# Reordering the twelve S1 T1 matmuls in one stage of a seven-product MLP kernel

## The chip, the cores and the metric

The kernel runs on one core of a Trainium2 chip. The metric is the device time of one execution in microseconds (us), lower is better. A change of 0.2% of this time is 1.15 us.

## The reference, cut to what matters

```python
# attention: linear attention with decay, in blocks; its output becomes x
x = attn_out.transpose(0, 2, 1, 3).reshape(1536, 512)
# first MLP ("layer 0"), d_model 512, d_ff 2048
h = np.maximum(x @ w_in, 0.0)
x = h * h @ w_out
# second MLP ("layer 1"), weights of the same shapes
h = x @ w_in2
out = np.maximum(0.01 * h, h) @ w_out2
```

Weights come as 64-bit floats and are turned into 32-bit ones on the chip.

## The kernel before, in words

Every 32-bit operand of a matmul is held as two parts, `hi` and `lo` (`split`: a cast on ScalarE, then a subtraction on VectorE), and a product is three matmuls: hi by hi, hi by lo, lo by hi. `three` (L562) issues them all, so nearly all TensorE rows of the trace have that line; the rows are told apart by the tiles they read.

The 1536 tokens are three tiles of 512 (t = 0, 1, 2). The hidden width of 2048 is cut into four stages (s = 0 to 3) of 512. A stage makes the hidden values of its 512 columns (`first`, the tiles g0 and g1 with parts h and l), multiplies them by its rows of the second weight, and adds the result into an accumulator in DRAM (`spill`). In the second and third stage of the first MLP, s = 1 and s = 2 (`seven`), the second matmul of the token tiles 0 and 1 is done by `second_pair` with seven block products in place of eight. The products are named by their operands: A11 B11, S1 T1, A12 B21, S4 B22, S2 T2, A22 T4, S3 T3. B and T are blocks of hidden values or differences of such blocks, A is a block of weights and S a sum of weight blocks (tile `sw` on the chip). Each product is done for two output halves p = 0, 1, and each half is six matmuls: two row blocks of hidden values (h = 0, 1) by three.

The order of the products on TensorE is the order in which the program is written. PSUM banks are named A, B, C, D per p. S1 T1 starts bank C, and S4 B22 adds to bank C later; in between, ScalarE must have copied bank C to SBUF (`keep`, L684), because the result of S1 T1 alone is wanted too. From SBUF the copy is added to DRAM by an accumulating DMA that POOL issues (L688), or stored by SP.

T1 is in g1: hi and lo of row block h = 0 come early, those of h = 1 come last, out of a chain on VectorE (L550, difference; L69, lo part) and ScalarE (L68, cast). After S1 T1, `late_split` writes T3 over T1 in the same tiles: a cast on ScalarE and a subtraction on VectorE for each h, at raised priority. The block T2 (tile `t4`, shown as `t`) is cast by L68 after VectorE's L455. ScalarE, VectorE and POOL get their order from a scheduler that goes by the program's dependences; each engine then runs its list strictly in order.

After the seven products, POOL also adds stored partial results to others in DRAM (L758): each waits for an earlier DMA of the same data. At the same time `converting` turns weights into 32-bit parts on ScalarE and VectorE (L115 to L138), each fed by a 1 MB load `raw` that SP issues as soon as VectorE's L123 has freed a buffer.

Of the kernel before, what the change touches and what calls it, by code (L numbers as in the profile page):

```python
# [19 lines left out]
def tile_retention_then_two_mlps(  # L20
# [16 lines left out]
    C = P  # L37
# [20 lines left out]
    def bank():  # L58
        return psum.tile([P, 512], F32, tag="ps", name="ps")

    def plain():
        return fp.tile([P, TT], F32, tag="f", name="f")

    def dma(dst, src):
        return nc.sync.dma_start(dst, src)

    def split(hi, lo, src):
        nc.scalar.copy(hi, src)  # L68
        nc.vector.tensor_tensor(out=lo, in0=src, in1=hi, op=ALU.subtract)  # L69
# [19 lines left out]
    wts, sums, opened = {}, {}, set()  # L89
# [470 lines left out]
    def three(ps, ops, start, stop, again=False):  # L560
        for n, (a, b) in enumerate(ops):
            nc.tensor.matmul(ps, a, b, start=start and n == 0, stop=stop and n == len(ops) - 1, skip_group_check=again)  # L562

    def first(l, s, t, ms=range(KF)):
        for m in ms:
            if m == 0:
                new_g(l, s, t)
            ghi, glo = g[t]
            hi, lo = wts[l, s, 0, m // 2]
            cs = slice(m % 2 * P, (m % 2 + 1) * P)  # L570
            ps = bank()
            ops = []
            for kk in range(KD):
                ops += [(hi[:, kk, cs], xhi[t][:, kk]), (hi[:, kk, cs], xlo[t][:, kk]), (lo[:, kk, cs], xhi[t][:, kk])]
            three(ps, ops[:6], True, False)
            yield True
            three(ps, ops[6:], False, True)
            if (l, s) in seven and t < 2:
                activate_for_seven(t, m, ps)
            elif (l, s) == stages[-1]:  # L580
                activate_last(t, m, ps)
                if m == KF - 1:
                    sums_last(t)
            else:
                activate(l, ps, plain(), ghi[:, m], glo[:, m])
            if t == 2 and m % 2:
                opened.add((*stages[stages.index((l, s)) + 1], 0, m // 2) if (l, s) != stages[-1] else None)
            yield True
# [93 lines left out]
    def keep(src, dst, first):  # L682
        f = plain()
        nc.scalar.copy(f, src)  # L684
        if first:
            dma(dst, f)
        else:
            nc.gpsimd.dma_start(dst, f, accum_op=ALU.add)  # L688
# [3 lines left out]
    def second_pair(s):  # L692
        partial = partials[s]
        (g0h, g0l), (g1h, g1l) = g[0], g[1]
        x = {
            "B11": [(g0h[:, 2 * h], g0l[:, 2 * h]) for h in range(2)],
            "B21": [(g0h[:, 2 * h + 1], g0l[:, 2 * h + 1]) for h in range(2)],
            "B22": [(g1h[:, 2 * h + 1], g1l[:, 2 * h + 1]) for h in range(2)],
            "T1": [(g1h[:, 2 * h], g1l[:, 2 * h]) for h in range(2)],
            "T2": [(tt[2][:, 0, h], tt[2][:, 1, h]) for h in range(2)],  # L700
        }
        ps = {}

        def product(p, where, a, b, start=True):
            if start:
                ps[p, where] = bank()
            ops = []
            for h in range(2):
                if a[0] == "A":
                    i, j = int(a[1]) - 1, int(a[2]) - 1  # L710
                    hi, lo = (w[:, j, (2 * p + i) * P:(2 * p + i + 1) * P] for w in wts[0, s, 1, h])
                else:
                    hi, lo = (sums[0, s, 1, h][:, part, int(a[1]) - 1, p] for part in range(2))
                bh, bl = x[b][h]
                ops += [(hi, bh), (hi, bl), (lo, bh)]
            three(ps[p, where], ops, start, True, not start)
            return ps[p, where]

        def kept(p, i, k):
            return spill[0][k][2 * p + i]  # L720

        def late_split(n, old, m):
            x[n] = x[old]
            with tc.high_priority(offset=400):
                for h in range(2):
                    split(*x[n][h], later[m(h)])

        both = range(2)
        for p in both:
            keep(product(p, "A", "A11", "B11"), partial[p]["P1"], True)  # L730
            yield True
        for p in both:
            keep(product(p, "C", "S1", "T1"), kept(p, 1, 1), False)
            yield True
        late_split("T3", "T1", lambda h: (1, 2 * h))
        for p in both:
            keep(product(p, "A", "A12", "B21", False), kept(p, 0, 0), False)
            yield True
        late_split("T4", "B21", lambda h: (0, 2 * h + 1))
        for p in both:  # L740
            keep(product(p, "C", "S4", "B22", False), kept(p, 0, 1), False)
            yield True
        for p in both:
            keep(product(p, "B", "S2", "T2"), partial[p]["P6"], True)
            yield True
        for p in both:
            keep(product(p, "D", "A22", "T4"), kept(p, 1, 0), False)
            yield True
        yield from first(0, s, 2)
        for p in both:  # L750
            keep(product(p, "B", "S3", "T3", False), partial[p]["P67"], True)
            yield True
        opened.add(("sums", 0, s + 1))
        for p in both:
            p1, p6, p67 = (partial[p][n] for n in ("P1", "P6", "P67"))
            for dst, src in ((p67, p1), (kept(p, 0, 1), p1), (kept(p, 0, 1), p6), (kept(p, 1, 0), p67),
                             (kept(p, 1, 1), p67)):
                nc.gpsimd.dma_start(dst, src, accum_op=ALU.add, max_dma_last_dim=TT)  # L758
# [136 lines left out]
    def stage(l, s):  # L895
        if (l, s) == (0, 0):
            parts = [first(l, s, t, range(2)) for t in range(NTILE)]
            parts += [first(l, s, t, range(2, 4)) for t in (0, 2, 1)]
            return parts + [second(l, s, t) for t in (2, 0, 1)]
        if l == 0:  # L900
            parts = [first(l, s, t, ms) for ms in (range(2), range(2, 4)) for t in range(2)]
        else:
            parts = [first_pair(s)]
        if (l, s) in seven:
            return parts + [second_pair(s), second(l, s, 2)]
        if (l, s) == (0, NS - 1):
            return parts + [second(l, s, 0), second(l, s, 1, (0, 2, 1)), first(l, s, 2), second(l, s, 1, (3,)),
                            second(l, s, 2)]
        if (l, s) == stages[-1]:
            return parts + [first(l, s, 2)] + [second_last(s, t) for t in range(NTILE)]  # L910
        return parts + [second(l, s, 0), first(l, s, 2), second(l, s, 1), second(l, s, 2)]
# [36 lines left out]
```

## Time and profile before

| what | value |
|---|---|
| device time, median of 3 runs (lowest, highest) | 573.77 us (573.05, 574.43) |
| profiled execution: device time, span of the trace | 575.28 us, 573.5 us |
| granted TensorE clock, mean | 0.999 |
| TensorE busy | 562.3 us, 98% of the span |
| VectorE, ScalarE, POOL busy | 441.1, 312.9, 112.5 us |
| TensorE idle after 100 us, all two waits | 1.5 us |

Times in rows count from the start of the span. In a row of a timeline the columns are start, duration, engine, line, operation, output<-inputs, count, and in brackets the idle time before it with what ended it. A row with "x2" merges two instructions, and the time between them is in its duration. Two matmuls in a row overlap, so durations are longer than the distance of their starts.

### The profile page before, as it was taken

Reading aid. Unit: us, or ns where it says so; the run is one execution under the profiler, and the core shown is the slowest. Engines: PE = TensorE matmul, PEld = TensorE weight load, DVE = VectorE, ACT = ScalarE, POOL = GpSimd, SP = SyncE. Lnnn points to the kernel's source line nnn. Section 1 sums busy time; section 2 is a strip of 40 time slices with the busy share of each in tenths; the row PEclk is TensorE's granted clock in tenths of the full one; section 3 lists DMA queues with packets and bytes.
Section 4 is the critical chain, followed back from the end, with each engine's and each line's share of the span. In section 5 each row is a group of like instructions: output and inputs, shape, how many; then the busy total and the mean of one; then the engine's idle time right before and its main releaser. Section 6 shows DMA issues by size and latency. Waiting matters only on the chain.

```text
span 573.5 us, 8321 instructions
## 1 busy us (share of the span) xinstructions
PE 562.3 (98%) x3171; PEld 473.3 (83%) x3171; DVE 441.1 (77%) x623; ACT 312.9 (55%) x494; POOL 112.5 (20%) x121
## 2 busy tenths in 40 slices
PE   7989999999999999999999999999999999999997
PEld 6879888888788887888888888888888888888897
DVE  3678999999927589498478999929875395918887
ACT  2344598556758677657538474543662375435610
POOL 3749100000044603434000000000203111220032
PEclk9999999999999999999999999999999999999999
DMA  8998434665589966999602225362439406460434
GB/s 176 233 216 174 151 125 142 223 191 176 181 148 146 137 193 155 218 242 200 194 8 88 76 69 196 110 209 74 64 84 240 54 7 141 59 89 2 155 140 147
DMA packets 80760, 80.77 MB, mean 141 GB/s; under 512 B 40264, under 2 KB 54608, under 8 KB 80720
## 3 DMA queue, kind: packets, MB, share of 16 engines
q1 hardware_dynamic: 62576, 62.01, 35.2%
q0 software_dynamic: 17472, 17.83, 22.7%
q8 instruction: 25, 0.41, 0.3%
q10 hardware_dynamic: 672, 0.39, 0.2%
q14 instruction: 15, 0.12, 0.1%
HBM read 55.05 MB, written 30.42 MB: 149 GB/s over the span
## 4 chain that ended last, share of the span: by engine, by line
PE 74%; DVE 11%; DMA 8%; ACT 3%; issue 2%; POOL 1%; SPq 0%; ACTq 0%; POOLq 0%; DVEq 0%
PE ps L562 69%; DMA raw<-in_moe_w_in 5%; DMA raw<-in_moe_w_out 2%; DVE rb L123 2%; DVE hb L119 2%; PE ps L298 1%; DVE hb L126 1%; ACT hb L115 1%; PE ps L315 1%; DVE rb L122 1%; DVE hb L116 1%; DMA q<-in_q 1%; PE ps L366 1%; PE ps L224 1%; PE ps L364 1%
## 5 line engine op out<-in xcount | busy, mean ns | idle before, releaser
L688 POOL DMA_DIRECT2D spill<-f x48 | 47.5, 1200 | 348.4 <-ACT f L684 348.3
L562 PE MATMUL ps<-xhi,w1h 128*128 128x512 f32 x288 | 112.2, 389 | 0.0
L562 PE MATMUL ps<-xlo,w1h 128*128 128x512 f32 x288 | 112.1, 389 | 0.0
L562 PE MATMUL ps<-xhi,w1l 128*128 128x512 f32 x288 | 112.0, 389 | 0.0
L684 ACT COPY f<-ps 128x512 f32<-128x512 f32 x84 | 48.4, 586 | 65.4 <-PE ps L562 64.5
L562 PEld LDWEIGHTS ps<-xhi,w1h 128*128 128x128 f32 x288 | 54.1, 188 | 11.3 <-issue 0.2
L562 PEld LDWEIGHTS ps<-xhi,w1l 128*128 128x128 f32 x288 | 54.1, 188 | 11.3
L562 PEld LDWEIGHTS ps<-xlo,w1h 128*128 128x128 f32 x288 | 54.1, 188 | 11.2
L115 ACT ACTIVATE hb<-raw 128x1024 f32<-128x1024 f32 x32 | 36.7, 1148 | 25.9 <-DMA raw<-in_moe_w_in 9.4
L479 DVE TENSOR_TENSOR g0l<-f,g0h 128x512 fp32r<-128x512 f32 x44 | 29.7, 687 | 25.4 <-ACT f L475 20.6
L138 DVE TENSOR_TENSOR w2l<-hb,w2h 128x1024 fp32r<-128x1024 f32 x16 | 19.5, 1223 | 29.5 <-ACT w2h L136 29.5
L562 PE MATMUL ps<-g0h,w2h 128*128 128x512 f32 x104 | 40.5, 389 | 0.0
L562 PE MATMUL ps<-g0l,w2h 128*128 128x512 f32 x104 | 40.5, 389 | 0.0
L562 PE MATMUL ps<-g0h,w2l 128*128 128x512 f32 x104 | 40.5, 389 | 0.0
L123 DVE SCALAR_TENSOR_TENSOR rb<-raw,rb 128x1024 f32<-128x1024 uint32 x32 | 39.4, 1232 | 0.4
L126 DVE TENSOR_TENSOR hb<-hb,rb 128x1024 f32<-128x1024 f32 x32 | 39.4, 1232 | 0.3
L562 PE MATMUL ps<-w2l,g0h 128*128 128x512 f32 (+1 forms) x104 | 39.6, 381 | 0.0
L562 PE MATMUL ps<-w2h,g0l 128*128 128x512 f32 (+1 forms) x104 | 39.6, 381 | 0.0
L562 PE MATMUL ps<-w2h,g0h 128*128 128x512 f32 (+1 forms) x104 | 39.6, 381 | 0.0
L119 DVE SCALAR_TENSOR_TENSOR hb<-raw,hb 128x1024 uint32<-128x1024 uint32 x32 | 39.1, 1221 | 0.4
L634 DVE TENSOR_TENSOR f<-ps,f 128x512 f32<-128x512 f32 x40 | 26.3, 685 | 10.7 <-PE ps L562 10.4
L116 DVE TENSOR_SCALAR hb<-hb 128x1024 f32<-128x1024 f32 x32 | 23.0, 718 | 12.4 <-ACT hb L115 12.1
(209 smaller groups left out, 1234.0 us busy)
## 6 DMA issues: line engine op xcount, KB each, us to landing
raw<-in_moe_w_in SPq DMA_DIRECT2D x16, 1024.0 KB, 5.7
raw<-in_moe_w_out SPq DMA_DIRECT2D x16, 1024.0 KB, 5.6
spill<-f POOLq DMA_DIRECT2D x48, 256.0 KB, 6.2
spill<-f SPq DMA_DIRECT2D x24, 256.0 KB, 2.5
k<-in_k SPq DMA_DIRECT2D x12, 256.0 KB, 4.9
q<-in_q SPq DMA_DIRECT2D x12, 256.0 KB, 5.1
v<-in_v SPq DMA_DIRECT2D x12, 256.0 KB, 5.1
f<-spill SPq DMA_DIRECT2D x12, 256.0 KB, 3.4
```

What stands on the lines that cost most here:

```text
L115: nc.scalar.activation(hf, w_hi.bitcast(F32), AF.Abs)
L116: yield ve.tensor_scalar(out=hf, in0=hf, scalar1=2.0 ** -15, scalar2=122368.0, op0=ALU.max, op1=ALU.min)
L119: yield ve.scalar_tensor_tensor(out=hb, in0=w_hi, scalar=0xC0000000, in1=hb, op0=ALU.bitwise_and, op1=ALU.bitwise_or)
L122: yield ve.tensor_scalar(out=rb, in0=hb, scalar1=0xFF800000, scalar2=None, op0=ALU.bitwise_and)
L123: yield ve.scalar_tensor_tensor(out=rf, in0=w_lo, scalar=2.0 ** -52, in1=rf, op0=ALU.mult, op1=ALU.mult)
L126: yield ve.tensor_tensor(out=hf, in0=hf, in1=rf, op=ALU.add)
L138: yield ve.tensor_tensor(out=lo, in0=hf, in1=hi, op=ALU.subtract)
L479: nc.vector.tensor_tensor(out=glo, in0=r, in1=ghi, op=ALU.subtract)
L562: nc.tensor.matmul(ps, a, b, start=start and n == 0, stop=stop and n == len(ops) - 1, skip_group_check=again)
L634: ve.tensor_tensor(out=out, in0=ps[h, where], in1=other, op=ALU.add)
L684: nc.scalar.copy(f, src)
L688: nc.gpsimd.dma_start(dst, f, accum_op=ALU.add)
```

## The change

For s = 1 alone, the twelve matmuls of S1 T1 are written in another order. Before, p = 0 had all its six, then p = 1, and each p was copied out after its own six. Now both banks are opened at once: three matmuls of h = 0 for p = 0, three for p = 1, then the two of h = 1 that read the hi part for p = 0, two for p = 1, and last the two that read the lo part of h = 1. Both copies come after that. The third stage (s = 2) keeps its order.

```diff
-        for p in both:
-            keep(product(p, "C", "S1", "T1"), kept(p, 1, 1), False)
-            yield True
+        if s == 1:
+            steps = {p: [] for p in both}
+            for p in both:
+                ps[p, "C"] = bank()
+                for h, (bh, bl) in enumerate(x["T1"]):
+                    ah, al = (sums[0, s, 1, h][:, part, 0, p] for part in range(2))
+                    steps[p] += [(ah, bh), (al, bh), (ah, bl)]
+            for lo, hi in ((0, 3), (3, 5), (5, 6)):
+                for p in both:
+                    three(ps[p, "C"], steps[p][lo:hi], lo == 0, hi == 6)
+                if lo == 0:
+                    yield True
+            for p in both:
+                keep(ps[p, "C"], kept(p, 1, 1), False)
+            yield True
+        else:
+            for p in both:
+                keep(product(p, "C", "S1", "T1"), kept(p, 1, 1), False)
+                yield True
```

On TensorE, at S1 T1 of the second stage, with `sw_1361` the weight sums of h = 0, `sw_1614` those of h = 1, and `ps_1777` bank C of p = 0; first before:

```order
L562 MATMUL ps_1777<-g1h_1604,sw_1361 128x512
L562 MATMUL ps_1777<-g1l_1605,sw_1361 128x512
L562 MATMUL ps_1777<-g1h_1604,sw_1361 128x512
L562 MATMUL ps_1777<-g1h_1604,sw_1614 128x512
L562 MATMUL ps_1777<-g1l_1605,sw_1614 128x512
L562 MATMUL ps_1777<-g1h_1604,sw_1614 128x512
L562 MATMUL ps_1788<-g1h_1604,sw_1361 128x512
L562 MATMUL ps_1788<-g1l_1605,sw_1361 128x512
```

and now, where bank C of p = 1 is `ps_1778`:

```order
L562 MATMUL ps_1777<-g1h_1604,sw_1361 128x512 x2
L562 MATMUL ps_1777<-g1l_1605,sw_1361 128x512
L562 MATMUL ps_1778<-g1h_1604,sw_1361 128x512 x2
L562 MATMUL ps_1778<-g1l_1605,sw_1361 128x512
L562 MATMUL ps_1777<-g1h_1604,sw_1614 128x512 x2
L562 MATMUL ps_1778<-g1h_1604,sw_1614 128x512 x2
L562 MATMUL ps_1777<-g1l_1605,sw_1614 128x512
L562 MATMUL ps_1778<-g1l_1605,sw_1614 128x512
```

The matmul that reads the lo part of h = 1 stood fifth and eleventh and now stands eleventh and twelfth.

On ScalarE, at the same place (`f_1784` or `f_1792` is the copy of bank C of p = 0, `g1h_1604<-f_1623` and `<-f_1717` the casts of T3, `t4_1654` that of T2):

```order
 L684 COPY f_1773<-ps_1766 128x512
-L684 COPY f_1784<-ps_1777 128x512
+L68 CAST g1h_1604<-f_1623 128x512
 L68 CAST t4_1654<-f_1744 128x512
-L68 CAST g1h_1604<-f_1623 128x512
 L68 CAST g1h_1604<-f_1717 128x512
-L684 COPY f_1795<-ps_1788 128x512
+L684 COPY f_1792<-ps_1777 128x512
+L684 COPY f_1795<-ps_1778 128x512
 L684 COPY f_1811<-ps_1755 128x512
 L68 CAST g0h_1557<-f_1595 128x512
```

The copy of bank C of p = 0 stood ahead of the three casts and now stands behind them.

## Rows read from the trace of the kernel before

**Rows 1.** The page, part 1: busy us (share of the span) and instructions by engine.

```profile
PE 562.3 (98%) x3171; PEld 473.3 (83%) x3171; DVE 441.1 (77%) x623; ACT 312.9 (55%) x494; POOL 112.5 (20%) x121
```

**Rows 2.** Waits of TensorE from 100 us on: total us, times, longest.

```profile
PE ps L562 <- DVE g1l L69: 1.5, 2, 0.9
```

**Rows 3.** Timeline of TensorE, second stage: S1 T1, A12 B21 from 157.47, S2 T2 last.

```profile
153.23 0.39 PE L562 MATMUL ps<-g1h,sw 128*128 128x512 f32 x1
...
153.68 0.93 PE L562 MATMUL ps<-g1h,sw 128*128 128x512 f32 x2
155.53 0.50 PE L562 MATMUL ps<-g1l,sw 128*128 128x512 f32 x1 [0.92 <-DVE g1l L69]
...
157.47 0.39 PE L562 MATMUL ps<-g0h,w2h 128*128 128x512 f32 x1
...
162.91 2.88 PE L562 MATMUL ps<-t,sw 128*128 128x512 f32 x12
```

**Rows 4.** Timeline of VectorE there: lo part of T1's h = 1, and L455.

```profile
154.79 0.68 DVE L69 TENSOR_TENSOR g1l<-f,g1h 128x512 fp32r<-128x512 f32 x1
...
156.96 0.69 DVE L455 TENSOR_TENSOR f<-f 128x512 f32<-128x512 f32 x1
```

**Rows 5.** Timeline of ScalarE there; 156.30 is the copy of bank C, p = 0.

```profile
153.44 0.62 ACT L68 CAST g1h<-f 128x512 fp32r<-128x512 f32 x1 [1.83 <-DVE f L550]
...
156.30 0.59 ACT L684 COPY f<-ps 128x512 f32<-128x512 f32 x1 [0.22 <-PE ps L562]
157.68 0.62 ACT L68 CAST t<-f 128x512 fp32r<-128x512 f32 x1 [0.79 <-DVE f L455]
158.21 1.14 ACT L68 CAST g1h<-f 128x512 fp32r<-128x512 f32 x2
159.25 1.06 ACT L684 COPY f<-ps 128x512 f32<-128x512 f32 x2
```

**Rows 6.** Timeline of TensorE, third stage: S1 T1, then A12 B21 from 221.20.

```profile
217.31 0.39 PE L562 MATMUL ps<-g1h,sw 128*128 128x512 f32 x1
...
219.25 0.49 PE L562 MATMUL ps<-g1l,sw 128*128 128x512 f32 x1 [0.58 <-DVE g1l L69]
...
221.20 0.40 PE L562 MATMUL ps<-g0h,w2h 128*128 128x512 f32 x1
```

**Rows 7.** Chain that ended last, 193 to 222 us: start, us, what.

```profile
200.24 8.20 DMA raw<-in_moe_w_in
...
218.59 0.61 DVE g1l L69
```

**Rows 8.** DMA queues, 200 to 204 us (first two) and 204 to 209 us.

```profile
q0 software_dynamic: 405, 0.70, 100.9%
q1 hardware_dynamic: 31, 0.06, 4.3%
...
q1 hardware_dynamic: 656, 1.64, 92.2%
```

**Rows 9.** Timeline of POOL, 150 to 210 us (DMAs that it issues).

```profile
157.21 1.03 POOL L688 DMA_DIRECT2D spill<-f  x1 [97.09 <-ACT f L684]
160.13 1.76 POOL L688 DMA_DIRECT2D spill<-f  x2 [1.90 <-ACT f L684]
...
170.04 1.05 POOL L758 DMA_DIRECT2D spill<-partial10P  x1 [5.18 <-DMA spill<-f]
...
185.92 1.02 POOL L758 DMA_DIRECT2D partial10P<-partial10P  x1 [6.46 <-DMA partial10P<-f]
```

**Rows 10.** Stores of partial10P issued at 155.1 and at 182.1: KB, us to landing.

```profile
partial10P<-f SPq DMA_DIRECT2D x1, 256.0 KB, 2.2
...
partial10P<-f SPq DMA_DIRECT2D x1, 256.0 KB, 3.6
```

**Rows 11.** Busy time by microsecond; the last three columns are clock, DMA share, GB/s.

```profile
161.00:162.00 1.00, 1.00 (x6) 0.81 (x5) 1.00 (x2) 1.00 (x3) 0.90 (x2) 1.00 0.82 47
162.00:163.00 1.00, 1.00 (x6) 0.83 (x5) 0.16 (x1) 0.34 (x1) 0.87 (x2) 1.00 0.71 96
163.00:164.00 1.00, 1.00 (x6) 0.84 (x5) 0.00 (x0) 0.59 (x1) 0.88 (x2) 1.00 1.17 172
```

## The prediction

> **What bounds the kernel now.** I read the page's busy times first: TensorE is busy 98% of the span [rows 1], so time is to be had only where it waits. The list of its waits after 100 us has one entry, two waits for the lo part of g1, 1.5 us in all [rows 2]. The timeline finds them at the same place of two stages, on the fifth matmul of S1 T1 [rows 3, 6]. The change is made at the first of them.
>
> A matmul has a pitch of 0.227 us there: 24 of them lie between 157.47 and 162.91 (5.44 / 24). S1 T1 of the second stage, twelve matmuls, should take 2.72 us and takes 157.47 - 153.23 = 4.24 us [rows 3]. So the place costs **1.52 us**: a late hi part (cast until 153.44 + 0.62 = 154.06 [rows 5], in the pair at 153.68), then the wait for the lo part (VectorE, until 154.79 + 0.68 = 155.47 [rows 4], TensorE goes on at 155.53, 0.06 later), and 0.13 us of slower pitch after it (eight matmuls from 155.53 to 157.47 are 1.94 us, not 1.81).
>
> **The change, part by part.** No matmul, copy or DMA is added or removed.
>
> *The new order on TensorE.* Ten matmuls now come before the first that reads the late lo part: it is due at 153.23 + 10 x 0.227 = 155.50. The hi part is needed at 153.23 + 6 x 0.227 = 154.59 and there since 154.06. VectorE and ScalarE do the same up to here, so the lo part comes at 155.47 and the matmul starts at 155.53 as before; the last one follows, and A12 B21 starts at 155.98, not 157.47. That is **1.49 us earlier**.
>
> *The copy of bank C, p = 0.* It stood on ScalarE at 156.30, ahead of three casts [rows 5]. Now it stands behind them, and one of these, the cast of T2, must wait for VectorE's L455, which ends at 156.96 + 0.69 = 157.65 [rows 4, 5] and is not moved by TensorE. So: T2's cast at 157.68, one cast of g1 at 158.21 (its pitch is (159.25 - 158.21) / 2 = 0.52), the copy at 158.73, done 0.59 later at 159.32. The other cast of g1 goes before T2's and fits in the 0.79 us in which ScalarE was idle. From 159.25 on the list of ScalarE stands where it stood.
>
> S4 B22 adds to bank C and cannot start before that copy is done. It is due at 155.98 + 12 x 0.227 = 158.70; it will start at 159.32 + 0.06 = 159.38, and pays the 0.13 of slow pitch again: **0.81 us of new wait**. With the 0.03 above, the place costs 0.84 in place of 1.52, and TensorE is **0.68 us early** from there on. Behind the waiting matmul stand the rest of S4 B22, then S2 T2 and A22 T4; the copies of their banks come later by as much, and nothing else waits for them there. Before, this copy had 3 us of cover (done by 156.9, needed at 160.19 or so, 162.91 less twelve pitches). T2 and T4 get no later by more than one 0.69 us subtraction on VectorE, and are needed over 2 us after they are ready; I cost them at nothing.
>
> *Does the gain reach the end?* There is one more wait, in the third stage: from 217.31 to 221.20 are 3.89 us for twelve matmuls, 1.17 more than 2.72 [rows 6]. While TensorE waits there, the end goes by what it waits for and not by when it came. The chain of waits says what that is: a weight load issued at 200.24 that takes 8.20 us, then ScalarE and VectorE without a gap up to L69 at 218.59 [rows 7]. The load is late because of DMA traffic: from 200 to 204 us the software queue (POOL's accumulating DMAs) is at 100.9% and the hardware queue with the load at 4.3%; from 204 on the load runs, at 92.2% [rows 8]. So the load lands about when POOL's traffic has drained, plus the same 4 us, whenever it is issued. An issue 0.68 us earlier stands in the same queue.
>
> The Trainium skill (DMA: Bandwidth & Descriptors, section Queues, rings and completion order) says that each DMA engine takes its queues in turn, packet by packet. By that the load would move from its issue on, beside POOL's traffic, and an earlier issue would land earlier; the sum would then be the 0.68 us gain. The trace does not agree with even turns: 4.3% beside 100.9%.
>
> *What POOL's traffic depends on.* Backward from the load: POOL's last group begins at 185.92, after 6.46 us of waiting for a store of partial10P [rows 9]. That store takes 3.6 us, while the same one in an idle moment takes 2.2 [rows 10], so it too stands behind POOL's traffic of 170 to 185. That begins at 170.04, after 5.18 us of waiting for a spill DMA to land [rows 9], one of six issued from 157.21 on. Their first is the copy of bank C, p = 0. It goes out at about 159.4 now, 2.2 us later; the other five follow copies that stand still, so they go out as before. What shifts is thus the moment at which six accumulating DMAs have drained, by d: **nothing**, if the idle DMA time of 161 to 163 takes up the first one's work, and at most its lateness less the unused share there, 2.2 - (0.18 + 0.29) = **1.7 us** [rows 9, 11]. By bytes, these two microseconds move 47 and 96 GB/s where the next moves 172, so 0.2 MB of 0.26 MB fit in, and some 0.06 MB at 172 GB/s, 0.35 us, stay over. I take **d = 0.4 us**, nearer to the bytes, since the queue's share counts waiting too.
>
> *The sum.* TensorE comes to the third stage 0.68 us early, waits there 1.17 + 0.68 + 0.4 = 2.25 us more than its pitch, and leaves it 0.4 us later than before. The rest of the program, 350 us without a wait [rows 2], follows. The trace has 573.5 us of span and 1.8 around it (575.3); both become 0.4 longer, 573.9 and 575.7. The profiled execution is 1.5 us above the median of 573.77, so the forecast for a median is 573.77 + 0.4 = **574.2 us**, no measurable change (0.2%, 1.15 us, is about what a measurement tells from nothing).
>
> **The rivals.**
>
> *The DMA chain moves with TensorE.* If the drain times at 170, 185 and 204 us follow TensorE's stores and loads and not POOL's first spill, everything shifts by -0.68: 573.1 us. For it: the load's issue, the third stage's activations and the store at 182.1 all come after TensorE's work. Against it: rows 8 and 10. The skill's rule on turns would also end here.
>
> *The copy does not hold.* If the copy of bank C is done before 158.70, the full 1.49 us come through, with a DMA chain that moves along: 572.3 us. Against it stands VectorE's L455, which ends at 157.65.
>
> *Slower: the backlog.* The late first spill is one mechanism that can turn it: each microsecond by which POOL's six spills drain later reaches the weight load, and through it the third stage, one to one. At d = 1.7 the time is 575.5 us; it counts as slower from d = 1.15 on. For it: the queue's share after 163 us is above 1, so work put there finds no room.
>
> *The change does nothing.* The stages cancel exactly: 573.8. This lies in the main case's bounds, and I give it no own range.
>
> **How the numbers follow.** Main case (d from 0 to 1.15): 0.55. Chain moves with TensorE: 0.25, of which 0.08 falls below 572.62 (the spread of runs is 1.4 us). Full gain: 0.08. Backlog over 1.15: 0.12. Faster by over 0.2%: 0.08 + 0.08 = 0.16. Slower: 0.12, and 0.01 of the main case by spread, 0.13. Within: 0.71. A range from 572.6 to 575.2 leaves out the full gain, a third of the second case's 0.25 and most of the backlog's 0.12, about 2 in 10 together once the backlog's near end is in; the main case alone runs from 573.4 to 575.0.
>
> **What the profile after will show.** Right: no wait for g1l in S1 T1 of the second stage; a wait of about 0.7 us for ScalarE's L684 ahead of S4 B22, with the copy starting at 158.7; A12 B21 at 156.0; S2 T2 at about 162.2, not 162.91; POOL's first spill near 159.4; the wait for g1l in the third stage above 1 us (0.58 now), with the weight load landing at or after 208.4. Wrong: the load lands before 208, or the third stage's wait stays at 0.58, or no wait for L684 appears. The forecast fails as a whole if six spills drain earlier or much later than reckoned, since their queue, not TensorE, then sets the end.

## The result, and the profile after

The changed kernel takes **577.30 us** (median of 7 runs, 575.56 to 579.14) where the kernel before, run beside it, takes 573.82 (7 runs, 572.81 to 575.72). The ratio is 1.0054, with an interval of 1.0041 to 1.0068: about 3.1 us slower by the ratio (the medians lie 3.5 apart). The forecast was 574.2, with a range up to 575.2.

The profiled execution after is the slowest of its seven: 577.4 us of span, 579.14 in all. It is read here against the profiled execution of before (573.5 of span), which was itself 1.5 us above its median.

The list of TensorE's waits from 100 us on (total us, times, longest), after; it answers to [rows 2]:

```profile
PE ps L562 <- ACT g1h L68: 2.0, 1, 2.0
PE ps L562 <- DVE g1l L69: 0.3, 1, 0.3
```

Both stand in the third stage. The second stage, where the change was made, has no wait left. Its timeline on TensorE, after (start, us, what; answers to [rows 3]):

```profile
153.50 0.61 PE L562 MATMUL ps<-g1h,sw 128*128 128x512 f32 x2
...
155.77 0.62 PE L562 MATMUL ps<-g1l,sw 128*128 128x512 f32 x2
156.22 0.39 PE L562 MATMUL ps<-g0h,w2h 128*128 128x512 f32 x1
...
158.94 0.42 PE L562 MATMUL ps<-g1h,sw 128*128 128x512 f32 x1
...
161.72 2.88 PE L562 MATMUL ps<-t,sw 128*128 128x512 f32 x12
```

S1 T1 takes 156.22 - 153.50 = 2.72 us, its bare pitch. S4 B22 starts at 158.94, as soon as A12 B21 is through. From the first S1 T1 to S2 T2 are 8.22 us, where before had 9.68. So TensorE is 1.46 us earlier here, and the change does what it says.

ScalarE's timeline there, after (answers to [rows 5]):

```profile
157.18 0.62 ACT L68 CAST t<-f 128x512 fp32r<-128x512 f32 x1 [1.09 <-DVE f L455]
157.71 0.62 ACT L68 CAST g1h<-f 128x512 fp32r<-128x512 f32 x1
158.23 1.56 ACT L684 COPY f<-ps 128x512 f32<-128x512 f32 x3
```

And POOL's, 150 to 225 us, after (answers to [rows 9]):

```profile
159.13 5.49 POOL L688 DMA_DIRECT2D spill<-f  x6 [98.70 <-ACT f L684]
171.18 1.05 POOL L775 DMA_DIRECT2D spill<-partial10P  x1 [6.57 <-DMA spill<-f]
...
187.16 1.02 POOL L775 DMA_DIRECT2D partial10P<-partial10P  x1 [6.89 <-DMA partial10P<-f]
```

The copy of bank C, p = 0, now starts at 158.23 and not at 156.30, behind T2's cast and one cast of g1. With it POOL's first spill goes out at 159.13, not 157.21, and POOL's next two groups (L758 is L775 now) start 1.1 and 1.2 us later than before (0.9 and 1.0 when each trace is counted from its first S1 T1 of the second stage).

The DMA queues from 199 to 204 us (packets, MB, share of 16 engines), after; they answer to [rows 8]:

```profile
q0 software_dynamic: 924, 0.81, 117.9%
q1 hardware_dynamic: 25, 0.05, 3.1%
```

And from 204 to 206 us, after:

```profile
q0 software_dynamic: 142, 0.26, 69.9%
q1 hardware_dynamic: 129, 0.26, 38.9%
```

In the kernel before, 199 to 204 us look alike (0.83 and 0.06 MB). The difference comes behind that: from 204 to 206 us its software queue has only 0.03 MB left to move, where after it still moves 0.26 MB beside the load.

The chain that ended last, 185 to 235 us (start, us, what), after; it answers to [rows 7]:

```profile
199.21 10.44 DMA raw<-in_moe_w_in
...
219.81 0.61 DVE g1l L69
220.42 0.04 issue
```

The weight load is issued 1.03 us earlier than before and lands 1.21 us later (209.65, before 208.44): the traffic of POOL ahead of it ends later. What hangs on it ends at 220.42, not 219.20.

TensorE's timeline in the third stage, after; it answers to [rows 6]:

```profile
214.58 0.50 PE L562 MATMUL ps<-g0l,w2h 128*128 128x512 f32 x1
...
216.54 0.40 PE L562 MATMUL ps<-g1h,sw 128*128 128x512 f32 x1
...
219.38 0.79 PE L562 MATMUL ps<-g1h,sw 128*128 128x512 f32 x1 [1.99 <-ACT g1h L68]
220.47 0.79 PE L562 MATMUL ps<-g1l,sw 128*128 128x512 f32 x1 [0.29 <-DVE g1l L69]
...
224.04 0.63 PE L562 MATMUL ps<-g0h,w2h 128*128 128x512 f32 x1
224.47 0.63 PE L562 MATMUL ps<-g0l,w2h 128*128 128x512 f32 x1
...
230.51 1.75 PE L562 MATMUL ps<-t,sw 128*128 128x512 f32 x7
```

The same stretch in windows (stretch, us, busy us and instructions of TensorE, granted clock, DMA share, GB/s), after:

```profile
218.00:219.00 1.00, 0.00 (x0) 1.00 0.00 0
219.00:220.00 1.00, 0.62 (x1) 0.67 0.00 0
...
222.00:225.00 3.00, 3.00 (x9) 0.50 0.96 302
...
226.00:227.00 1.00, 1.00 (x5) 0.92 1.14 262
```

Two things are to be seen. The fifth matmul starts at 220.47 and, without a wait, was due at 216.54 + 4 x 0.227 = 217.45: late data cost **3.02 us**. And after the idle time the granted clock is 0.50, the lower of TensorE's two levels (1.2 and not 2.4 GHz), until about 226: matmuls start 0.43 us apart and not 0.227. From the first S1 T1 to S2 T2 are 230.51 - 216.54 = 13.97 us; without waits it is 36 pitches, 8.16. So 5.81 us are lost, and 5.81 - 3.02 = **2.79 us** of them after the data had come, to the lower clock.

That is nearly the whole of it. Between these two executions, measured from the first S1 T1 of the second stage, S1 T1 of the third stage is reached 1.04 us earlier (63.04 for 64.08), the way from there to S2 T2 takes 4.63 us more (13.97 for 9.34), and the end comes 3.63 later (423.90 for 420.27). Of the 1.46 us of the second stage 0.42 is gone before S1 T1 of the third: in the product ahead of it the matmul at 214.58 was due at 214.31, and the ones behind it start a little further apart than before. It reads g0l, which VectorE's L547 finished at 214.52, in the same chain behind the weight load. So the late load takes its first 0.42 us there.

### The profile page after: what moved, and what is told of

It is laid out like the page before. It is cut to its first block, busy times and chain, and to the rows that moved or that the text cites. A ratio compares the mean times of both kernels' runs of the same rounds, so it can differ in the third digit from the quotient of the medians.

```text
span 577.4 us, 8323 instructions
## 1 busy us (share of the span) xinstructions
PE 566.0 (98%) x3171; PEld 475.9 (82%) x3171; DVE 441.5 (76%) x623; ACT 314.0 (54%) x494; POOL 112.5 (19%) x121
## 4 chain that ended last, share of the span: by engine, by line
PE 91%; DMA 4%; DVE 1%; ACT 1%; issue 1%; SPq 1%; POOL 1%; ACTq 0%; POOLq 0%
PE ps L562 84%; DMA raw<-in_moe_w_in 3%; PE ps L298 2%; PE ps L315 2%; PE ps L366 2%; PE ps L364 1%; PE ps L339 1%; DMA q<-in_q 1%; SPq L65 1%; ACT qT L302 0%; POOL kd L333 0%; POOL qS L308 0%; ACT hb L115 0%; DVE hb L119 0%; DVE rb L123 0%
## 5 line engine op out<-in xcount | busy, mean ns | idle before, releaser
L684 ACT COPY f<-ps 128x512 f32<-128x512 f32 x84 | 48.8, 586 | 68.0 <-PE ps L562 67.6
L115 ACT ACTIVATE hb<-raw 128x1024 f32<-128x1024 f32 x32 | 36.8, 1151 | 25.7 <-DMA raw<-in_moe_w_in 10.0
```

Of the source, the lines that this page charges most:

```text
L115: nc.scalar.activation(hf, w_hi.bitcast(F32), AF.Abs)
```

## The experiments

The theory: the matmul order is sound and saves time; what costs is the place of bank C's copy, p = 0, on ScalarE. It starts POOL's spills late, POOL's traffic then drains late, the load behind it lands late, and the third stage waits (with a lower clock at times). The rivals: the order itself costs; or the wait alone does not, and it is all the clock. In the short diffs "hold" is an argument that keeps an instruction at the place in its engine's order where the code has it.

**The late copy alone** (e2): the matmul order of before, with the two copies of bank C behind the casts of T3.

```diff
-        for p in both:
-            keep(product(p, "C", "S1", "T1"), kept(p, 1, 1), False)
-            yield True
-        late_split("T3", "T1", lambda h: (1, 2 * h))
+        if s == 1:
+            for p in both:
+                product(p, "C", "S1", "T1")
+                yield True
+            late_split("T3", "T1", lambda h: (1, 2 * h), hold)
+            for p in both:
+                keep(ps[p, "C"], kept(p, 1, 1), False, hold)
```

> The matmul order of before, in all stages; in the second stage alone ScalarE's copies of bank C are put behind the casts of T2 and T3, as the change has them, so POOL's first accumulating DMA goes out near 159.3 instead of 157.2. Theory (late DMA chain): POOL's DMAs drain about 1.2 us later, the weight load of the third stage lands about 1.2 us later, S1 T1 there waits 1.2 us longer; so 575.0 us if the clock holds, and up to 577.6 if it falls as in the changed kernel. Rival (the interleaved matmul order itself costs time): same as before, 573.8 us, as the order is not used.

Measured: 574.98 us (11 runs) against 573.61 for before, ratio 1.0025 (1.0009 to 1.0041). The late copy makes even the old order slower. The waits of TensorE in its profile:

```profile
PE ps L562 <- DVE g1l L69: 1.5, 2, 0.9
PE ps L562 <- ACT g1h L68: 1.0, 1, 1.0
```

POOL's timeline in it (L767 is the group that was L758):

```profile
159.50 5.48 POOL L688 DMA_DIRECT2D spill<-f  x6 [99.81 <-ACT f L684]
170.76 1.05 POOL L767 DMA_DIRECT2D spill<-partial10P  x1 [5.78 <-DMA spill<-f]
```

ScalarE's first reading of the load, L115, whose start tells when that landed:

```profile
208.85 1.12 ACT L115 ACTIVATE hb<-raw 128x1024 f32<-128x1024 f32 x1 [3.93 <-DMA raw<-in_moe_w_in]
```

The 0.9 us of the old order is still there, and a wait for g1h of 1.0 us has come in the third stage. The first spill, 157.21 before, is out at 159.50; the load is read at 208.85. Counted from the first S1 T1 of the second stage, that is 6.71 us for 3.98 and 56.06 for 55.22.

**The new order with the early copy** (e1): the changed kernel with both copies of bank C held ahead of T2's cast and of T3's.

```diff
             for p in both:
-                keep(ps[p, "C"], kept(p, 1, 1), False)
+                keep(ps[p, "C"], kept(p, 1, 1), False, tc.keep_in_program_order)
+            with tc.high_priority(offset=400):
+                split(*deferred.pop(), tc.keep_in_program_order)
             yield True
...
-                split(tt[2][:, 0, h], tt[2][:, 1, h], later[1, m])
+                if (s, h) == (1, 1):
+                    deferred.append((tt[2][:, 0, h], tt[2][:, 1, h], later[1, m]))
+                else:
+                    split(tt[2][:, 0, h], tt[2][:, 1, h], later[1, m])
...
-        late_split("T3", "T1", lambda h: (1, 2 * h))
+        late_split("T3", "T1", lambda h: (1, 2 * h), tc.keep_in_program_order if s == 1 else lambda step: None)
```

> The changed matmul order in the second stage, with ScalarE's two copies of bank C pinned ahead of the casts of T2 and T3 there. POOL's first two accumulating DMAs then go out near 157 and 158, not 159.1 and later. Theory (the loss comes from the late first DMA): POOL's DMAs drain no later than in the kernel before, the weight load of the third stage lands no later, and the loss of 3.5 us goes: 573 to 574 us, below 573 if the gain of 1.5 us in the second stage comes through, 574 or a little more if TensorE, early by 1.5 us, waits so long in the third stage that its clock falls. Rival (loss is not in the copy's place): 577 us as in the changed kernel.

Measured: 572.93 us (12 runs) against 573.89, ratio 0.9994 (0.9982 to 1.0007). The loss is gone. In its profile (every line past the edit has a number 2 to 7 higher, L689 is the copy, L782 the group of POOL) TensorE has no wait from 100 us on. ScalarE's timeline, the copy of bank C, p = 0, and the load's first reading:

```profile
155.39 0.59 ACT L689 COPY f<-ps 128x512 f32<-128x512 f32 x1 [0.73 <-PE ps L567]
...
205.41 1.12 ACT L115 ACTIVATE hb<-raw 128x1024 f32<-128x1024 f32 x1 [1.91 <-DMA raw<-in_moe_w_in]
```

POOL's timeline:

```profile
156.30 1.94 POOL L693 DMA_DIRECT2D spill<-f  x2 [96.71 <-ACT f L689]
160.29 3.52 POOL L693 DMA_DIRECT2D spill<-f  x4 [2.05 <-ACT f L689]
168.59 1.05 POOL L782 DMA_DIRECT2D spill<-partial10P  x1 [4.78 <-DMA spill<-f]
```

The first spill is out at 156.30, and the load is read 3.46 us earlier than in the profile after, counted from the first S1 T1 of the second stage (52.71 for 56.17). So the two halves of the change come apart: old order with a late copy, slower; new order with an early copy, not slower.

**Less of POOL's traffic** (e4 on the changed kernel, e5 on the one before): the ten accumulating DMAs of the second stage that add partial sums are left out, so the sums lack that part.

```diff
+                if s == 1:
+                    continue
```

> The changed kernel without the ten accumulating DMAs by which POOL adds stored partial products to others in the second stage (that part of the sum is left out; the third stage's stay). Theory: the weight load then meets an almost empty queue and lands in time, the third stage does not wait, and the gain of the new order comes through: about 1.2 to 1.5 us below the same kernel with the old order. Rival (new order is slower by itself): not below it.

> The kernel before without the same ten accumulating DMAs of the second stage. Theory: only the third stage's wait goes, 1.17 us: 573.8 - 1.2 = 572.6 us. Rival (the load is bound by its own issue and not by POOL's traffic): the wait stays, 573.8 us.

Measured: e4 573.07 us (12 runs), ratio 0.9987 (0.9973 to 1.0001); e5 574.10 (11 runs), ratio 1.001 (1.0002 to 1.0019). Without that traffic the changed kernel is no longer slower, though its copy is as late as ever; the order, late copy included, is worth about 574.10 - 573.07 = 1.0 us there (1.3 by the two ratios, each of which has an interval of about 0.1% to either side). The hardware queue from 199 to 204 us in e5:

```profile
q1 hardware_dynamic: 482, 0.97, 59.5%
```

ScalarE's L115 in e4:

```profile
203.55 1.16 ACT L115 ACTIVATE hb<-raw 128x1024 f32<-128x1024 f32 x1
```

The hardware queue moves 0.97 MB in the five microseconds in which it moves 0.05 after and 0.06 before, and the load in e4 has landed by 203.55. The expectation for e5 was missed: before does not gain by losing the traffic. The next run says why in part; what makes e5 slightly slower than before stays open.

**Before and after again** (b2 and a2, one execution each; a3 with 12 runs): no edit.

> The kernel before, for a second profile: how far the landing of the third stage's weight load and the wait there differ between executions. If the profiled execution was typical: wait near 1.2 us again, POOL's drain 16.8 us after the start of S1 T1.

> The changed kernel, for a second profile. Theory: POOL's first DMA again 1.6 us later after the start of S1 T1 than in the kernel before, the drain about 1 us later, the wait in the third stage above 2 us and the granted clock at half for some us behind it.

> The changed kernel once more, timed beside the next three. Executions so far gave 575 to 579 us. Theory: always slower than before, by 1.2 us and more: 575 to 577.3, the more the lower the mean granted clock of the execution is.

Measured: b2 573.09 us, a2 574.98, a3 575.44 (574.11 to 578.48) against 573.62, ratio 1.0043 (1.0026 to 1.0061). The second execution of before is not like the first. Its waits of TensorE from 100 us on:

```profile
PE ps L562 <- DVE g1l L69: 0.3, 1, 0.3
```

POOL's first spill in it:

```profile
156.18 1.03 POOL L688 DMA_DIRECT2D spill<-f  x1 [96.18 <-ACT f L684]
```

And ScalarE's L115:

```profile
205.98 1.13 ACT L115 ACTIVATE hb<-raw 128x1024 f32<-128x1024 f32 x1 [1.40 <-DMA raw<-in_moe_w_in]
```

It has no wait in the third stage, 0.3 us in the second where the first had 0.92, and its load is read 2.3 us earlier, counted from the first S1 T1 of the second stage. The second execution after, TensorE's timeline in the third stage:

```profile
217.88 0.49 PE L562 MATMUL ps<-g1h,sw 128*128 128x512 f32 x1 [1.16 <-ACT g1h L68]
218.97 0.50 PE L562 MATMUL ps<-g1l,sw 128*128 128x512 f32 x1 [0.59 <-DVE g1l L69]
```

A window of it:

```profile
220.00:222.00 2.00, 2.00 (x10) 1.00 0.87 289
```

It waits 1.75 us in two pieces and keeps its clock. The third (a3, 578.0 us in the profiled execution) waits 1.86 and 0.59 us and does not keep it; the same window:

```profile
220.00:222.00 2.00, 1.54 (x4) 0.58 0.47 109
```

So the wait is in each execution after that was profiled, the lower clock in two of three. The lower clock that was expected in a2 was a miss. In a3 the copy of bank C, p = 0, also holds up TensorE in the second stage, at the first matmul of S4 B22:

```profile
159.37 0.50 PE L562 MATMUL ps<-g1h,sw 128*128 128x512 f32 x1 [0.35 <-ACT f L684]
```

The twelve runs of a3 lie in two groups, seven from 574.11 to 575.50 and five from 577.07 to 578.48. Three of the first group are less than 1.2 us above before, so "always" in the expectation was a miss too. The mean granted clock of each run is on record: 0.997 to 1.000 in the first group, 0.990 to 0.996 in the second. The means of the groups differ by 0.006; as an estimate from these means, that is 3.3 us of full clock lost in 576, and the groups lie 2.9 us apart. So in a3 the lower clock goes with the second group.

**Extra matmuls in the place of the wait** (e3 twelve, e7 seven): the changed kernel, with matmuls put ahead of the waiting one in the third stage, into a bank that is overwritten afterwards.

```diff
+                    for _ in range(12):
+                        nc.tensor.matmul(ps[1, "C"], *ops[0], start=True, stop=True, skip_group_check=True)
```

> The changed kernel, with twelve extra matmuls in the third stage, after the first three of S1 T1, into bank C of p = 1 before that bank is started (their results are overwritten); they take the place of TensorE's idle time. Theory (a third of the loss is the late load, the rest is TensorE's clock, which falls to half after the long wait): the wait stays but the clock stays at 1.00, so about 573.8 + 1.2 = 575.0 us. Rival (the rest is lost elsewhere, not by the clock): 577.3 us as in the changed kernel.

> The changed kernel with seven extra matmuls (1.6 us) in the third stage's wait, in place of twelve (2.7 us), results overwritten as there. Twelve are longer than the wait of some executions, so they cost time of their own. Theory (late load plus falling clock): about 574.5 us, 0.5 to 1 below the twelve, and 1 to 2.5 below the changed kernel beside it. Rival (the clock plays no part): not below the changed kernel.

Measured: e3 575.35 us (7 runs), ratio 1.0034 (1.0022 to 1.0047); e7 576.51 (6 runs), ratio 1.0048 (1.0032 to 1.0063). With 2.72 us of work added, e3 takes no longer than a3 (575.35 and 575.44). Its profile, of the fastest of its seven runs (574.46), has no wait in the third stage; TensorE's timeline, L759 the added ones:

```profile
215.60 2.88 PE L759 MATMUL ps<-g1h,sw 128*128 128x512 f32 x12
218.32 0.39 PE L562 MATMUL ps<-g1h,sw 128*128 128x512 f32 x1
```

The clock is whole, in a window of twelve microseconds:

```profile
214.00:226.00 12.00, 12.00 (x54) 1.00 0.59 157
```

The run e7 was a miss, 2 us above what was expected. Two of its six runs take 574.03 and 574.62, as expected, and four 576.45 to 576.87; the profiled one was of the first kind, without a wait and with its full clock. The other four were not profiled; their mean clocks (0.994 to 0.997, and 0.997 in the two) hardly tell them apart. So the share of the clock in the median loss is not settled by these runs; it is read from single executions and from the two groups of a3.

**The new order in both stages, copies where they fall** (e8): the condition on the stage is dropped.

```diff
-        if s == 1:
+        if True:
```

> The new order in the second and in the third stage, copies left where the scheduler puts them (late). Theory: the weight load stays late, and of the third stage's wait the part for the lo part goes (0.6 us of idle and up to 0.7 us of lost pitch), that for the hi part stays: 574 to 575 us, still not below the kernel before. Rival (the order in the third stage alone brings what the run with both stages and copies first brought): 572.7 us.

Measured: 575.28 us (5 runs), ratio 1.0034 (1.0022 to 1.0047). POOL's first spill is 6.92 us behind the first S1 T1, the load lands late, and the third stage waits, though its order asks for the late part last. S4 B22 also waits for the copy of bank C (L684), 0.35 us in the second stage and 1.17 in the third. The order does not cure the late copy.

**The new order in both stages, copies first** (e6, and e9 the same again): e1's edit in both stages, on top of e8's (the condition on T2's cast becomes h == 1).

> As the run with copies first, and the third stage in the same order with its copies first as well. There the matmul that needs the last lo part also stands behind ten others, so of the third stage's wait only what the late hi part causes is left. Theory: another 0.5 to 1.2 us below the run with copies first, about 572.5 us. Rival (the wait only moves from the lo part to the hi part, which come 1.1 us apart): same as the run with copies first.

> New order in both stages with copies first, a second time, since its gain is little over what can be told: 572.7 us, 0.1 to 0.4% below the kernel before. If the first result was chance: within 0.1%.

Measured: e6 572.65 us (12 runs), ratio 0.9976 (0.996 to 0.9992); e9 572.47 (11 runs), ratio 0.998 (0.9972 to 0.9989). This version beats both kernels, by about 1.2 us against before. Its profile has no wait of TensorE from 100 us on, and the load is there in time, by ScalarE's L115:

```profile
205.04 1.13 ACT L115 ACTIVATE hb<-raw 128x1024 f32<-128x1024 f32 x1 [1.32 <-DMA raw<-in_moe_w_in]
```

**All of them side by side**, us from the first S1 T1 of the second stage, each from one profiled execution; a loss is what a stage takes from its S1 T1 to S2 T2 above 8.16 us, in the third stage with the extra matmuls of e3 and e7 included.

| kernel | loss, second stage | first spill | POOL's first add of a partial sum | load read | loss, third stage |
|---|---|---|---|---|---|
| before | 1.52 | 3.98 | 16.81 | 55.22 | 1.18 |
| b2 | 0.63 | 3.08 | 15.46 | 52.88 | 0 |
| e1 | 0 | 3.60 | 15.89 | 52.71 | 0.17 |
| e6 | 0 | 3.60 | 15.46 | 52.11 | 0 |
| e9 | 0.03 | 3.61 | 16.06 | 52.33 | 0 |
| mean of five, copy early | | 3.57 | 15.94 | 53.05 | |
| after | 0.06 | 5.63 | 17.68 | 56.17 | 5.81 |
| a2 | 0.28 | 5.81 | 16.92 | 55.13 | 2.32 |
| a3 | 1.10 | 6.63 | 18.76 | 56.64 | 4.53 |
| e2 | 1.32 | 6.71 | 17.97 | 56.06 | 3.82 |
| e3 | 0 | 5.42 | 16.74 | 54.26 | 2.72 |
| e7 | 0.30 | 5.83 | 16.77 | 54.15 | 1.69 |
| e8 | 1.37 | 6.92 | 18.67 | 56.46 | 2.78 |
| mean of seven, copy late | | 6.14 | 17.64 | 55.55 | |

On the means, a first spill that is 2.56 us later goes with an add that is 1.70 later and a load that is 2.50 later. Single executions overlap: the load of before, at 55.22, lies among the late ones, and those of e3 and e7 are earlier than it.

## Why the prediction was wrong

The mechanism was named, as a rival of one chance in eight: the late first spill reaches the third stage through the weight load. Point by point:

- *The new order on TensorE*: right. A12 B21 starts 2.72 us after the first S1 T1 (forecast 2.75).
- *The copy of bank C, p = 0*: right in its place, and in its price on TensorE where VectorE is as late as in the profiled before. In the profile after T2's cast starts 3.68 us behind the first S1 T1 (before: 4.45), the copy starts at 158.23 (forecast 158.73), and S4 B22 loses 0.06 us by it. In a3 and e8 the cast starts 4.68 and 4.98 us behind, and S4 B22 loses 0.73 and 0.69; the forecast was 0.81. POOL's first spill is at 159.13 (forecast 159.4). The larger cost is on POOL's side.
- *TensorE is early*: by 1.04 us at the third stage against the profiled before, and 1.0 by e4 against e5; the forecast was 0.68. The 1.52 us that the order was to save belong to one execution, though: in b2 the same place loses 0.63, and after, a2 and a3 lose 0.06, 0.28 and 1.10 in the second stage.
- *"I take d = 0.4 us, nearer to the bytes"*: this is the step that failed, a term of the right kind and too small. The free DMA time of 161 to 163 us did not take up the first spill's work. At the point where d was defined, when the six spills have drained and POOL goes on, it is 0.87 in the profiled pair (17.68 for 16.81, with the first spill 1.65 us late) and 1.65 between the means of the three profiles of after and the two of before (first spill 2.49 late). The upper bound from the shares, 1.7 for a spill 2.2 late, was the nearer guess; that the numbers nearly meet is partly chance, as the lateness was not the same. At the load the shift is 0.95 in the pair and 1.93 between these means. A low rate, as at 161 to 163 us before, need not mean room. After, POOL issues its six spills one behind the other from 159.13, and still the microseconds from 160 to 162 move little (us, busy us and instructions of POOL, clock of TensorE, DMA share, GB/s):

```profile
160.00:161.00 1.00, 1.00 (x3) 1.00 0.61 33
161.00:162.00 1.00, 1.00 (x3) 1.00 0.73 53
```

  From 158 to 160 us, where before has DMA shares of 0.39 and 0.89, after has 0.03 and 0.00. Of the 1.65 us by which the first spill is late, 0.87 had not been made up when the six had drained. What limits the rate of these DMAs was not measured.
- *"waits there 1.17 + 0.68 + 0.4 = 2.25 us"*: the 1.17 belonged to one execution. In b2 it is nothing, so the third stage of an ordinary execution of before stands near the edge of waiting, and the sum had to start from 0 to 1.17 and not from 1.17. The lateness of the data after is 2.18 (a2), 2.88 (a3) and 3.02 us (profile after), so the wait's size came out about right for a wrong reason: too large a start, too small a shift.
- *"The rest of the program, 350 us without a wait, follows"*: it does, but not at the old clock. The lower clock, 2.79 us in the profile after and 1.65 in a3, stood in no term of the sum. It is the second thing that failed: a wait of over 2 us was priced at its length alone.
- *The range*: the main case's "573.4 to 575.0" is not what d from 0 to 1.15 gives, which is 573.8 to 574.9. With d = 1.65 the sum gives 575.4, outside the main case and above the range.

Put together from the profiles: from the first S1 T1 of the second stage to S2 T2 of the third, before and b2 take 73.42 and 71.35 us, and after, a2 and a3 take 77.01, 73.32 and 76.35. On the mean that is 3.2 us more, as much as the times of these executions differ (577.4 for 574.2), so the change costs its time in this stretch. Within it the second stage loses 0.6 us less on the mean, and the third 3.6 more: its data come 2.2 to 3.0 us late where before lost 0 to 1.2, and the clock takes 0 to 2.8 on top. The two measurements of the changed kernel are, by their ratios, 3.1 and 2.5 us slower.

**What is shown and what is not.** Shown, by e1 and e2 from both sides, is that the copy's place, ahead of the casts or behind them, makes the loss and the order does not; e4 and e5 show that POOL's traffic stands between the copy and the load. The part of the lower clock is read from the traces of after and a3 against a2 and from the two groups of a3, not isolated: e3 fits it and e7 does not. Why e5 is 0.1% slower than before is open.

The rival in which the DMA chain moves with TensorE fell: the load is issued earlier and lands later. The Trainium skill (DMA: Bandwidth & Descriptors, section Queues, rings and completion order), by which each DMA engine serves its queues in turn, would have had the load move from its issue on. The traces do not agree while POOL's accumulating DMAs are queued: 3.1% beside 117.9% after, 3.9% beside 106.1% in a2, 1.1% beside 115.0% in e2. Where the backlog is smaller the two share: 48.0% beside 58.0% in e1. At the end of the backlog after, from 204 to 206 us, they move 129 and 142 packets, and there the trace agrees with turns. What keeps the load from its packets before that was not measured.

## What to carry to other kernels

A reordering on one engine also moves what the other engines read from it: follow the copy out of the bank to the DMA that it issues, and that DMA to what queues behind it, tens of microseconds on. Where a wait is short and ends on a DMA, profile the kernel before a second time before its length goes into a sum, since one execution may have 1.2 us there and the next none. When a matmul order is made tolerant of late data, keep the copy that drains its bank ahead of the casts that can wait; only with that, and in both stages, did the order pay (ratios 0.9976 and 0.998; 0.9994 with the copies first in one stage, 1.0054 and 1.0043 with the late copy).

## What the runs showed of the hardware

- TensorE's granted clock fell to the lower level for about 6 us (0.50 in the profile after, 220 to 226 us) after 1.99 and 0.29 us of idle time that followed a busy stage. Waits of 1.16 and 0.59 us left it at 1.00 in a2. After 1.86 and 0.59 us in a3, and after 1.04 and 0.58 us in e2, it was at the lower level for about 3 us; in e2 it is 0.50 from 221 to 223 us, which shows in the mean of this window:

```profile
216.00:222.00 6.00, 4.37 (x14) 0.84 0.32 79
```

  So the same length of wait goes either way, and a price for a wait of 1 to 2 us has an upper end well above its length. The Trainium skill (TensorE: Matmul & The Clock Gate, section Part 1: The HAM clock gate) gives the clock two states, 1.2 GHz when idle and 2.4 GHz when busy. The 0.50 agrees with the lower of the two.
- A weight load of 1 MB on the hardware queue moved 0.05 MB in 5 us while accumulating DMAs filled the software queue, and 0.97 MB in the same 5 us with ten of them left out (e5). In e5 it was issued at 199.53 and moved 0.10 MB from 200.5 to 201 us; after, issued at 199.21, it moved nothing before 203.
